# Nine attention steps of a fused attention and expert kernel: outputs placed one step later, between the next step's transposes and scores

## The chip, the cores and the metric

The kernel runs on one core of one Trainium2 chip. The metric is the device time in microseconds (us) of one execution, as the median of several runs. The engines are named as in the profile: PE is TensorE (its weight loads are PEld), DVE is VectorE, ACT is ScalarE, POOL is GpSimd, SP is SyncE, which issues most of the DMAs.

## The reference

Attention over 4 batches, 8 heads, 768 tokens and a head size of 64; each token sees the keys less than 16 places away and one summary key (a maximum) and one summary value (a mean) for each block of 32 tokens. Behind it stands a network on the 3072 tokens with 512 features each.

```python
k_sum = k.reshape(B, H, nb, block, D).max(axis=3)
v_sum = v.reshape(B, H, nb, block, D).mean(axis=3)
scores_all = np.concatenate([scores_l_m, scores_s], axis=-1)   # local with a mask, summaries + log(32)
a = np.exp(scores_all - max); a = a / (sum(a) + 1e-9)
attn = np.matmul(a, np.concatenate([v, v_sum], axis=2))
x = attn as (3072, 512)
h = (x @ w1) * (x @ w2) @ w3
out = h @ w_out
```

## The kernel before

**Two kinds of work share the core.** The attention is cut into 24 *steps*: 6 units of 512 tokens times 4 pairs of heads, step s being unit s // 4 and pair s % 4. The network is a long *stream* of matmuls of 128x512 (the *big* matmuls), which a generator hands out in order; `run(columns)` issues them until a given count of columns is reached. In the profile they are `mm` (L167) until about 245 us and `ln` (L731) from then on. The weights of the `ln` part are loaded into tiles `ws` (L776, L861, L867), some of them sums of weights that the kernel itself works out (`wr`, `sp`, cast by ACT at L682) and writes to DRAM (`wS`, `pS`, L688).

**A step of attention.** PE multiplies queries and keys into two PSUM banks, one for each head: `sc`, 32 small matmuls (L408). DVE adds the mask and takes the maxima (`reduce`, L422). ACT takes the exponential with the sums (`expose`, L436), then the inverse and `normalize` (L446). PE transposes the result `sm` into two banks `tp`, 16 small matmuls (L466). `evacuate` copies them into SBUF as `pt`: the first by ACT (L471), the second by ACT (L473), in two lumps by DVE (L475). PE multiplies `pt` by the values `v` into one bank `po`, 32 small matmuls (L486), and ACT copies that out as `xraw` (L507), or as `x` for the first 8 steps.

**PSUM.** Banks are handed out by tags, in turns. The tag `sc` has four: the scores take two, `po` takes one (`SPARE`, L457), and from lump 16 on `tp` takes two as well (L1176), since the two `tp` banks then belong to the stream. A new tile in a bank waits until the tile before it there has been read.

**A lump.** The first 8 steps are started by a plan written by hand (`PLAN`). The others go by `lump(p)`, p from 8 to 25 (L1168), which mixes three steps into a share of the stream. For p at its middle values a lump holds, in the order of PE: the transposes of step p−2; the scores of step p; 18 big matmuls; the outputs of step p−2; the rest of its big matmuls, up to `UP_TO[p]`. The order of PE and POOL is the written one; for ACT and DVE the written order holds among the attention instructions (the `manual_schedule` of L1177 and L1188), and a scheduler places those of the stream between them; SP is placed by the scheduler.

**Loads of a step.** `fetch(p + 1)` loads queries and keys (L373, L375). `fetch_values(p)` (L1199), behind the outputs of step p−2, loads the values of step p (`v`, L358), and the next lump's `fetch_means` (L1174) adds the means of the blocks (`v<-vS`, L391).

Of the kernel before, what the change touches and what calls it, by code (L numbers as in the profile page):

```python
# [91 lines left out]

HOMES = "TSTSTTTT"
BANKS = "STTTSTST"
SOONER = 400
RING = 5

# [18 lines left out]
def attention_moe(ctx, tc, qG, kW, kT, vP, vW, vB, mask, w1, w2, w3T, wo, out, outT):  # L116
# [52 lines left out]
    def aligned(shape, **more):  # L169


        n = math.prod(shape[1:])
        step = 32 if more["bufs"] % 4 == 0 else 64
        t = sb.tile([shape[0], -(-n // step) * step], F32, **more)[:, :n]
        return t.rearrange("p (a b) -> p a b", b=shape[2]) if len(shape) == 3 else t
# [85 lines left out]
    def fold_weights(order):  # L261
        acc = {}
        for i, j in order:
# [15 lines left out]
            def store(i=i):  # L279
                done = acc.pop(i)[:, :DO]  # L280
                with tc.high_priority(offset=SOONER):
                    nc.scalar.copy(wp[i][:, 0], done)
# [64 lines left out]
    def batches(u):  # L347

        for b in range(B):
            at, to = max(0, b * BLOCKS - u * NBLK), min(NBLK, (b + 1) * BLOCKS - u * NBLK)  # L350
            if at < to:
                yield b, slice(at, to), to - at

    def load_values(u, p):


        v = sb.tile([P, 2, NBLK, P], F32, name="v", bufs=2)
        nc.sync.dma_start(v, vW[u, p])  # L358
        return v
# [27 lines left out]
    def fetch_means(u, p, v):  # L387
        for b, blocks, n in batches(u):
            for g, at in enumerate((CUT, CUT - 64)):
                src = vS[b][32 * p : 32 * p + NB]  # L390
                nc.sync.dma_start(v[at : at + NB, g, blocks], src.unsqueeze(1).broadcast_to([NB, n, P]))  # L391
# [7 lines left out]
    def scores(q, k):  # L399

        sc = [ps.tile([P, 512], F32, name="sc", bufs=4) for _ in range(2)]
        for i in range(NBLK):
            for g in range(2):
                for h in range(2):
                    rows = slice(h * D, (h + 1) * D)
                    nc.tensor.matmul(  # L408
                        sc[h][64 * g : 64 * g + 64, i * KR : (i + 1) * KR],
                        lhsT=q[rows, i * P + 64 * g : i * P + 64 * g + 64],  # L410
                        rhs=k[rows, i, 64 * g : 64 * g + KR],
                        start=True,
                        stop=True,
                    )
        return sc
# [41 lines left out]
    SPARE = {"tag": "sc", "bufs": 4}  # L457

    def transposes(sm, **more):

        tp = [ps.tile([P, 512], F32, name="tp", **more or {"bufs": 2}) for _ in range(2)]
        for j in range(NI):
            for g in range(2):
                rows = slice(64 * g, 64 * g + 64)
                to, p = tp[g][:KR, j * 64 : j * 64 + 64], sm[rows, j]
                nc.tensor.transpose(to, p, ident[rows, rows])  # L466
        return tp

    def evacuate(tp, second="V"):
        pt = [sb.tile([KR, U], F32, name="pt", bufs=6) for _ in range(2)]  # L470
        nc.scalar.copy(pt[0], tp[0][:KR, :U])  # L471
        if second == "A":
            nc.scalar.copy(pt[1], tp[1][:KR, :U])  # L473
        else:
            nc.vector.tensor_copy(pt[1], tp[1][:KR, :U])  # L475
        return pt

    def outputs(pt, v, **more):

        po = ps.tile([P, 512], F32, name="po", **more or {"tag": "tp", "bufs": 2})  # L480
        for i in range(NBLK):
            for g in range(2):
                at = (2 * i + g) * 64
                for h in range(2):
                    cols = slice(h * D, (h + 1) * D)
                    nc.tensor.matmul(  # L486
                        po[cols, at : at + 64],
                        lhsT=v[:KR, g, i, cols],
                        rhs=pt[g][:, (h * NBLK + i) * 64 : (h * NBLK + i + 1) * 64],
                        start=True,  # L490
                        stop=True,
                    )
        return po
# [34 lines left out]
    def gate(fs, x, hs, wide=False):  # L528
# [5 lines left out]
        for c0, c1 in parts:  # L534
            for f in fs:
                k, cols = f * P // FQ, slice(f * P % FQ, f * P % FQ + P)
                for w in range(2):
# [14 lines left out]
                    if w == 0 and c1 == NC:  # L552
                        g = sb.tile([P, U], F32, name="g", tag="pt", bufs=6)
                        with tc.high_priority(offset=SOONER):
                            nc.scalar.copy(g, a)  # L555
                if c1 == NC:
                    if f % 2 == 0:
                        pair_of_h[0] = sb.tile([P, 2, 2, U], F32R, name="h", tag="ring", bufs=RING)
                    h = pair_of_h[0][:, f % 2]
                    with tc.high_priority(offset=SOONER):  # L560
                        nc.vector.tensor_tensor(g, acc[f, 1][:, :U], g, ALU.mult)
# [5 lines left out]
    def project(u, ts, hs, parts):  # L567
        acc = {t: ps.tile([P, 512], F32, name="mm", **bank(u == 1)) for t in ts}
        for fs in parts:
            for t in ts:  # L570
# [10 lines left out]
                if f == NF - 1:  # L581
                    o = sb.tile([P, DO], F32, name="o", tag="pt", bufs=6)
                    with tc.high_priority(offset=SOONER):
                        nc.scalar.copy(o, acc[t][:, :DO])
# [5 lines left out]
    NS = NU * NPAIR  # L590
# [125 lines left out]
    def lanes(n, o, weights_of, moving_of, steps, evacuated, tags, between=None, last=None):  # L716

        banks = [ps.tile([P, 512], F32, name="ln", tag=tag, bufs=bufs) for tag, bufs in tags]
        for at, k in enumerate(o.ids):
            stationary_of = yield from weights_of(at, k)  # L720
            for i in range(n):
# [3 lines left out]
                for c in range(steps):  # L725
# [13 lines left out]
                    if c < steps - 1:  # L739
                        yield 3 * U  # L740
                with tc.high_priority(offset=SOONER):
                    evacuated(at, k, i, banks[i][:, :U])
# [128 lines left out]
    def project_fast(n, whole):  # L871
        parts = []

        def between(at, j):
            with tc.high_priority(offset=SOONER // 2):
                if j < 3 and at + 2 < NK:
                    for work in whole.moving(at + 2):
                        next(work, 0)
            if n + 1 < NSU and j == 3 and at in (4, 5):
                moving_x(n + 1, at - 4)  # L880
# [99 lines left out]
    def tend():  # L980


        some = False
        for works in (tasks, background):
            while works:
                n = next(works[0], 0)
                if n > 0:
                    return True
                if n < 0:
                    break  # L990
                works.pop(0)
                some = True
        return some

    def run(columns):

        while given[0] < columns:
            n = next(stream, 0)
            if n <= 0:
                if n == 0 or not tend():  # L1000
                    return
                continue
            given[0] += n
            if given[0] >= tended[0]:
                tended[0] = given[0] + 4 * U
                tend()

    def place(s):
        return divmod(s, NPAIR)

    inputs, values, sms = {}, {}, {}
# [5 lines left out]
    def fetch_values(s):  # L1017
        if s < NS:
            values[s] = load_values(*place(s))
# [9 lines left out]
    def begin(s):  # L1029
        u, p = place(s)  # L1030
        sm = sb.tile([P, NI, KR], F32, name="sm", tag="wf", bufs=5)
        mx = aligned([P, 3, NI], name="mx", bufs=4)
        sms[s] = sm, mx
        return u, sm, mx, scores(*inputs.pop(s))
# [47 lines left out]
    def step(s):  # L1082
# [11 lines left out]
        yield  # L1094
        pt = evacuate(transposes(sms.pop(s)[0], **(SPARE if BANKS[s] == "S" else {})), SECOND[s])
        yield
# [40 lines left out]
    def finish_step(p, pt, **more):  # L1137
        u, c = place(p)
        po = outputs(pt, values.pop(p), **more)
        if u < 2:  # L1140
            keep_x(po, xs[u])
        else:
            keep_raw(po, u, c)
# [14 lines left out]
    for p in range(2 * NFIRST + 2, NS + 2):  # L1158
# [6 lines left out]
        15: [lambda: flow_in(4), lambda: moving_x(1, 2)],  # L1165
        17: [lambda k=k: moving_x(1, k) for k in range(3, NK)],
    }
    def lump(p):  # L1168

        if p == NFIRST:  # L1170
            load_batch()
            fill(p)
        elif p <= NS:
            fetch_means(*place(p - 1), values[p - 1])  # L1174
            fetch(p + 1)
        more = SPARE if p >= 2 * NFIRST else {}  # L1176
        with tc.manual_schedule(engines={engines.Activation, engines.DVE}):  # L1177
            tp = transposes(sms.pop(p - 2)[0], **more)
            pt = evacuate(tp, 'V' if p in (12,13,) else 'A')
            b = begin(p) if p < NS else None  # L1180
            if b:
                u, sm, mx, sc = b
                reduce(u, 0, sc, sm, mx)
                if p > NFIRST + 1:
                    expose(0, sm, mx)
                    reduce(u, 1, sc, sm, mx)
        run(given[0] + (24 if p == NFIRST + 1 else 18) * U)
        with tc.manual_schedule(engines={engines.Activation, engines.DVE}):  # L1188
            finish_step(p - 2, pt, **SPARE)
            if b:  # L1190
                if p <= NFIRST + 1:
                    expose(0, sm, mx)
                    reduce(u, 1, sc, sm, mx)
                expose(1, sm, mx)
                invert(mx)
                normalize(sm, mx)
            fill(p + 1)
            reduce_batch()
        fetch_values(p)  # L1199
        for work in EXTRA.get(p, ()):  # L1200
            work()
        run((given[0] + UP_TO[p]) / 2)
        load_batch()
        run(UP_TO[p])

    with tc.manual_schedule(engines=MANUAL):
        for p in range(NFIRST, NS + 2):
# [70 lines left out]
```

## Time and profile before

| | us |
|---|---|
| median of 3 runs | 505.18 |
| lowest and highest of them | 504.29, 505.75 |
| profiled execution, its own time | 507.58 |
| span of the profiled execution | 505.8 |

The mean granted clock of TensorE was 0.993 of full speed. The page gives the busy time of each engine over the span and the share of each in the chain that ended last. The chain is a list of pieces (start, duration, engine, tile and line); where PE is never idle, it is PE's own row of work. Lump 8 and the following ones begin where `tp` stands in it: lump 12 at 197.88 us, 16 at 243.93, 17 at 253.83, 20 at 300.12, 21 at 314.85, 22 at 330.32, 25 at 374.87; behind them comes only the stream.

### The profile page before, as it was taken

What the parts mean: (1) busy time and instruction counts of PE and PEld (TensorE: products, weight loads), DVE (VectorE), ACT (ScalarE), POOL (GpSimd) and SP (SyncE); (2) the same over time, 40 slices, a digit from 0 to 9 for tenths busy, and PEclk for the clock granted to TensorE, in tenths of its full rate; (3) what the DMA queues carried; (4) which work ended last, traced back from release to release, by engine and by line L of the source; (5) the groups of instructions that cost most, each with busy time, mean ns of one, the idle gap of its engine ahead of it and who ended that gap; (6) DMA issues with size and microseconds to landing.
All of it is one profiled execution on the core that took longest, in us unless ns stands there. A gap on an engine that the chain in (4) does not pass through costs nothing.

```text
span 505.8 us, 10295 instructions
## 1 busy us (share of the span) xinstructions
PE 487.9 (96%) x3756; PEld 391.7 (77%) x3756; DVE 366.3 (72%) x885; ACT 325.2 (64%) x890; POOL 43.8 (9%) x78
## 2 busy tenths in 40 slices
PE   1989999999999999999999999999999999999997
PEld 1658777888877777778777788777887888888886
DVE  5888987896845698994689865589977029129972
ACT  4977888893726788887897478547865421422710
POOL 2014301511320001000000000000000000000000
PEclk9979999999999999999999999999999999999999
DMA  8999769994975788899789877796858765656752
GB/s 319 407 398 358 279 230 404 409 399 191 319 279 173 266 278 278 270 327 364 262 287 328 294 288 224 289 329 182 250 192 243 225 192 190 202 180 200 212 186 101
DMA packets 52146, 136.65 MB, mean 270 GB/s; under 512 B 5120, under 2 KB 16128, under 8 KB 51072
## 3 DMA queue, kind: packets, MB, share of 16 engines
q1 hardware_dynamic: 50944, 133.90, 76.1%
q10 hardware_dynamic: 1152, 2.10, 1.1%
q8 instruction: 30, 0.49, 0.4%
q14 instruction: 20, 0.16, 0.1%
HBM read 107.47 MB, written 28.51 MB: 269 GB/s over the span
## 4 chain that ended last, share of the span: by engine, by line
PE 89%; ACT 4%; DMA 4%; DVE 1%; issue 0%; SPq 0%; DVEq 0%; ACTq 0%
PE ln L731 46%; PE mm L167 31%; PE po L486 5%; PE sc L408 4%; PE tp L466 3%; DMA wraw<-in_wo_dram 2%; DMA wS<-sp 2%; ACT wf L216 1%; DMA v<-in_vW_dram 1%; ACT wraw L224 1%; ACT w L246 1%; PE ln L167 1%; PE means L335 1%; ACT sm L446 0%; ACT sm L452 0%
## 5 line engine op out<-in xcount | busy, mean ns | idle before, releaser
L731 PE MATMUL ln<-xT,ws 128*128 128x512 f32 x672 | 157.1, 392 | 0.0
L731 PEld LDWEIGHTS ln<-xT,ws 128*128 128x128 f32 x672 | 124.9, 188 | 27.7 <-issue 1.1
L167 PE MATMUL mm<-x,w 128*128 128x512 f32 x384 | 91.9, 395 | 0.8 <-ACT g L555 0.8
L167 PEld LDWEIGHTS mm<-x,w 128*128 128x128 f32 x384 | 70.8, 188 | 17.8 <-ACT g L555 1.2
L436 ACT ACTIVATE sm<-sm,mx 128x120 f32<-128x120 f32 x192 | 73.9, 390 | 9.1 <-DVE mx L422 8.9
L731 PE MATMUL ln<-hT,ws 128*128 128x512 f32 x324 | 75.6, 392 | 0.0
L751 DVE TENSOR_TENSOR tmp<-ln,tmp 128x512 f32<-128x512 f32 x51 | 35.1, 688 | 52.0 <-PE ln L731 37.7
L731 PEld LDWEIGHTS ln<-hT,ws 128*128 128x128 f32 x324 | 60.3, 188 | 12.9 <-DVE hT L163 0.2
L167 PE MATMUL mm<-w,w 128*128 128x512 f32 x192 | 51.5, 422 | 13.5 <-ACT w L246 9.0
L650 ACT CAST hT<-hr 128x512 fp32r<-128x512 f32 x56 | 32.1, 621 | 42.7 <-DVE hr L808 35.1
L167 PEld LDWEIGHTS mm<-w,w 128*128 128x128 f32 x192 | 37.8, 202 | 24.4 <-ACT w L246 9.8
L422 DVE CUSTOM_DVE_ANT_0 sm<-sc,mask_sb 128x120 f32<-128x120 f32 x192 | 42.3, 277 | 7.4 <-PE sc L408 7.3
L167 PE MATMUL mm<-wp,h 128*128 128x512 f32 x192 | 46.0, 394 | 0.0
L446 ACT ACTIVATE sm<-sm,mx 128x120 f32<-128x120 f32 x128 | 39.0, 389 | 6.1 <-DVE mx L442 6.1
L167 PEld LDWEIGHTS mm<-wp,h 128*128 128x128 f32 x192 | 35.5, 188 | 8.0 <-issue 0.5
L163 DVE TENSOR_TENSOR hT<-hr,hT 128x512 fp32r<-128x512 f32 x56 | 35.5, 685 | 7.1 <-ACT hT L650 6.8
L436 ACT ACTIVATION_READ_ACCUMULATOR sm<-sm,mx 128x1 f32 x192 | 37.0, 192 | 0.0
L395 POOL COPY k<-ks 128x96 f32<-128x96 f32 (+1 forms) x32 | 13.5, 435 | 226.7 <-DMA k<-in_kW_dram 189.8
L486 PEld LDWEIGHTS po<-pt,v 120*64 120x64 f32 x768 | 24.5, 138 | 8.0 <-issue 4.5
L163 DVE TENSOR_TENSOR sp<-wr,sp 128x512 fp32r<-128x512 f32 x24 | 16.5, 696 | 16.7 <-ACT sp L682 16.6
L216 ACT ACTIVATE wf<-wraw 128x1024 f32<-128x1024 f32 (+1 forms) x24 | 23.4, 984 | 7.2 <-DMA wraw<-in_wo_dram 5.1
L486 PE MATMUL po<-pt,v 120*64 120x64 f32 x768 | 27.7, 225 | 0.2 <-ACT pt L473 0.2
(67 smaller groups left out, 570.5 us busy)
## 6 DMA issues: line engine op xcount, KB each, us to landing
ws<-wS SPq DMA_DIRECT2D x56, 512.0 KB
v<-in_vW_dram SPq DMA_DIRECT2D x24, 512.0 KB
wraw<-in_w_dram SPq DMA_DIRECT2D x8, 1024.0 KB
wS<-sp SPq DMA_DIRECT2D x16, 512.0 KB
ws<-pS SPq DMA_DIRECT2D x16, 512.0 KB
k<-in_kW_dram SPq DMA_DIRECT2D x20, 368.0 KB
wraw<-in_w3T_dram SPq DMA_DIRECT2D x7, 1024.0 KB
raw<-in_kT_dram SPq DMA_DIRECT2D x16, 392.0 KB
```

Of the source, the lines that this page charges most:

```text
L163: eng.tensor_tensor(dst, src, hi.bitcast(F32), ALU.subtract)
L167: nc.tensor.matmul(acc, lhsT=a, rhs=b, start=first and i == 0, stop=last and i == len(terms) - 1)
L216: nc.scalar.activation(f[:, some], words[:, some, 1].bitcast(F32), AF.Prelu, scale=2.0**-112, alpha=-(2.0**32),)
L408: nc.tensor.matmul(sc[h][64 * g : 64 * g + 64, i * KR : (i + 1) * KR], lhsT=q[rows, i * P + 64 * g : i * P + 64 * g + 64], rhs=k[rows, i, ...
L422: nc.vector.tensor_tensor_reduce(out=sm[:, j], in0=sc[h][:, i * KR : (i + 1) * KR], in1=mask_sb[:, 0 if blk == 0 else 2 if blk == BLOCKS - ...
L436: nc.scalar.activation(sm[:, j], sm[:, j], AF.Exp, bias=mx[:, 0, j : j + 1], scale=-1.0, accum_out=mx[:, 1, j : j + 1])
L446: nc.scalar.activation(sm[:, j], sm[:, j], AF.Copy, scale=mx[:, 2, j : j + 1])
L466: nc.tensor.transpose(to, p, ident[rows, rows])
L486: nc.tensor.matmul(po[cols, at : at + 64], lhsT=v[:KR, g, i, cols], rhs=pt[g][:, (h * NBLK + i) * 64 : (h * NBLK + i + 1) * 64], start=Tru ...
L650: nc.scalar.copy(dst[0], src)
L731: nc.tensor.matmul(banks[i][:, :U], lhsT=x, rhs=y, start=c + j == 0 and k in o.first, stop=c == steps - 1 and j == 2 and k in o.last, skip ...
L751: nc.vector.tensor_tensor(parts[to], got, parts[more], ALU.add)
```

## The change

`MERGED` names nine steps: 9 to 13 and 16 to 19. For these `lump(s + 2)` makes the transposes and `pt` as before, but keeps `pt`; the outputs are made in `lump(s + 3)`, behind that lump's transposes and copies and ahead of its scores. The other steps from 8 on (8, 14, 15, 20 to 23) and the last two of the first eight, 6 and 7, keep their place in the middle of the lump. So lump 11 and lump 18 have no outputs; lump 16 has those of step 13 at its start and of step 14 in its middle; lump 22 those of step 19 and of step 20. `fetch_values(s + 2)` follows the lump part in which step s was finished, so the values of steps 11 to 15 and 18 to 21 are loaded a lump later; the list `fresh` has the means follow at the start of the next lump.

```diff
+MERGED = (9, 10, 11, 12, 13, 16, 17, 18, 19)
...
+    fresh, kept_for_later = [], {}
+
     def lump(p):
...
-            fetch_means(*place(p - 1), values[p - 1])
+            while fresh:
+                s = fresh.pop(0)
+                fetch_means(*place(s), values[s])
             fetch(p + 1)
         more = SPARE if p >= 2 * NFIRST else {}
+        finished = []
         with tc.manual_schedule(engines={engines.Activation, engines.DVE}):
             tp = transposes(sms.pop(p - 2)[0], **more)
             pt = evacuate(tp, 'V' if p in (12,13,) else 'A')
+            if p - 3 in kept_for_later:
+                finish_step(p - 3, kept_for_later.pop(p - 3), **SPARE)
+                finished.append(p - 3)
             b = begin(p) if p < NS else None
...
         run(given[0] + (24 if p == NFIRST + 1 else 18) * U)
         with tc.manual_schedule(engines={engines.Activation, engines.DVE}):
-            finish_step(p - 2, pt, **SPARE)
+            if p - 2 in MERGED:
+                kept_for_later[p - 2] = pt
+            else:
+                finish_step(p - 2, pt, **SPARE)
+                finished.append(p - 2)
...
-        fetch_values(p)
+        for s in finished:
+            fetch_values(s + 2)
+            if s + 2 < NS:
+                fresh.append(s + 2)
```

On PE the two lumps 19 and 20 stood like this before (each row is a run of like matmuls: line, output and inputs, shape, count):

```order
L466 MATMUL tp<-ident,sm 120x64 x16
L408 MATMUL sc<-k,q 64x120 x16
L731 MATMUL ln<-xT,ws 128x512 x18
L486 MATMUL po<-pt,v 64x64 x16
L731 MATMUL ln<-xT,ws 128x512 x36
L466 MATMUL tp<-ident,sm 120x64 x16
L408 MATMUL sc<-k,q 64x120 x16
L731 MATMUL ln<-xT,ws 128x512 x18
L486 MATMUL po<-pt,v 64x64 x16
L731 MATMUL ln<-xT,ws 128x512 x33
```

and stand like this now, all lines being one higher up to the lump:

```order
L467 MATMUL tp<-ident,sm 120x64 x16
L487 MATMUL po<-pt,v 64x64 x16
L409 MATMUL sc<-k,q 64x120 x16
L732 MATMUL ln<-xT,ws 128x512 x54
L467 MATMUL tp<-ident,sm 120x64 x16
L487 MATMUL po<-pt,v 64x64 x16
L409 MATMUL sc<-k,q 64x120 x16
L732 MATMUL ln<-xT,ws 128x512 x51
```

The outputs have moved ahead of the scores, and the two runs of big matmuls have become one; the big matmuls are the same, in the same order. (These lists show 16 for the 32 matmuls that the profile counts in sc and po.)

In lump 16 PE has these waits now, at the end of tp and at the start of po and of sc (numbers tell tiles apart; the square brackets name what the instruction waits for):

```order
L467 MATMUL tp_3046<-ident_64,sm_2758 120x64
L487 MATMUL po_3067<-pt_2896,v_2836 64x64 [waits DMAHW2_49,DMAHW5_49,DVE_49,PE_49]
...
L409 MATMUL sc_3087<-k_2873,q_2872 64x120 [waits DMAHW4_49,DMAHW7_49,Activation_49,Pool_49]
L409 MATMUL sc_3088<-k_2873,q_2872 64x120 [waits Activation_49]
L409 MATMUL sc_3087<-k_2873,q_2872 64x120
L409 MATMUL sc_3088<-k_2873,q_2872 64x120
```

The second scores matmul waits for ACT's copy of the first tp tile of the same lump, whose bank it takes; it has the same wait in lumps 19 to 22. On ACT, from the end of lump 20 to the middle of lump 21, this was the order before:

```order
L441 ACTIVATE mx<-mx 128x8
L446 ACTIVATE sm<-sm,mx 128x120 x8
L682 CAST sp<-wr 128x512
L471 COPY pt<-tp 120x512
L473 COPY pt<-tp 120x512
L682 CAST sp<-wr 128x512
L436 ACTIVATE sm,mx<-sm,mx 128x120 x4
L507 COPY xraw<-po 128x512
L436 ACTIVATE sm,mx<-sm,mx 128x120 x4
```

and this is it now:

```order
L442 ACTIVATE mx<-mx 128x8
L447 ACTIVATE sm<-sm,mx 128x120 x8
L683 CAST sp<-wr 128x512 x2
L472 COPY pt<-tp 120x512
L474 COPY pt<-tp 120x512
L508 COPY xraw<-po 128x512
L437 ACTIVATE sm,mx<-sm,mx 128x120 x8
```

Both casts of `sp` now stand ahead of the two copies, and the copy of po stands ahead of the exponentials instead of between them. The first of the two casts overwrites a tile whose DMA to `pS` must have landed.

## The prediction

> **What bounds the kernel now.** I read the page first: how busy each engine is, the granted clock, and by what the chain that ended last is made up.
>
> ```profile
> PE 487.9 (96%) x3756; PEld 391.7 (77%) x3756; DVE 366.3 (72%) x885; ACT 325.2 (64%) x890; POOL 43.8 (9%) x78
> ...
> PEclk9979999999999999999999999999999999999999
> ...
> PE 89%; ACT 4%; DMA 4%; DVE 1%; issue 0%; SPq 0%; DVEq 0%; ACTq 0%
> ```
>
> TensorE (PE) is busy 96% of the span at full clock and makes 89% of the chain. The next question is whether it waits anywhere near the changed steps. The view of PE's waits from 120 to 400 us has one row:
>
> ```profile
> PE mm L167 <- ACT g L555: 0.8, 1, 0.8
> ```
>
> One wait of 0.8 us; from there to the last matmul PE runs on. So in the changed stretch time can only be won by making PE's own row of work shorter, and each wait that the change gives PE lengthens the kernel one for one. What PE does in a lump is in the chain (start, duration, what); here are lump 16 (its tp at 243.93), the po of lump 17, the second half of lump 19, lump 20 and the end:
>
> ```profile
> 243.93 0.61 PE tp L466 x16
> ...
> 249.87 1.08 PE po L486 x32
> 250.95 2.94 PE ln L731 x12
> ...
> 259.84 1.08 PE po L486 x32
> ...
> 291.73 8.38 PE ln L731 x36
> 300.12 0.61 PE tp L466 x16
> 300.73 0.98 PE sc L408 x32
> 301.71 4.34 PE ln L731 x18
> 306.06 1.08 PE po L486 x32
> 307.14 7.70 PE ln L731 x33
> 314.85 0.61 PE tp L466 x16
> ...
> 380.89 118.69 PE ln L731 x522
> ```
>
> A lump is transposes (tp), scores (sc), 18 big matmuls, outputs (po), and the rest of the big matmuls, each starting where the last ended. Two runs behind po differ only in length: 36 take 8.38 us, 12 take 2.94 us, so one big matmul costs (8.38 − 2.94) / 24 = 0.2267 us, and a run behind po has 8.38 − 36 × 0.2267 = 0.22 us more than its matmuls. The run behind sc has 4.34 − 18 × 0.2267 = 0.26 us more. I call this the edge: what it costs PE to go between small and big matmuls.
>
> **The change part by part.** *The merged run.* In nine lumps po leaves the middle of the big matmuls and goes between tp and sc. No matmul is removed. Two runs (4.34 + 8.38 = 12.72 us) become one of 54: 54 × 0.2267 + 0.26 = 12.50 us. That saves 0.22 us a step and 9 × 0.22 = 1.98 us in all.
>
> *What po costs in its new place.* It has tp ahead of it and sc behind it. The early part of the program has one of these two edges:
>
> ```profile
> 51.63 1.08 PE po L486 x32
> 52.71 0.98 PE sc L408 x32
> 53.70 2.27 PE mm L167 x9
> ```
>
> Here po with sc behind it takes 1.08 us and sc 0.98 us, as elsewhere, so that edge adds nothing. tp with po behind it is not in this trace. Its bounds: nothing, or the idle time that the weight loads show where PE goes from sc to big matmuls, 0.16 us:
>
> ```profile
> 301.64 3.99 PEld L731 LDWEIGHTS ln<-xT,ws 128*128 128x128 f32 x18 [0.16 <-issue]
> ```
>
> So the saving of a step lies between 0.22 − 0.16 = 0.06 and 0.22 us, or 0.5 to 2.0 us for nine. I take 0.22, since small matmuls follow one another in the nearest row (po to sc) without a price.
>
> *A new wait for PSUM banks.* The tag "sc" has four banks. From lump 16 on tp takes two of them, sc two and po one, five in a lump. Before, the order tp, tp, sc, sc, po let po come round to the first bank of tp, long after its copy. With tp, tp, po, sc, sc it is the second scores bank that comes round to the first bank of tp of the same lump, and its first matmul, the second of the scores, waits until ScalarE (ACT) has copied it out (L471). What covers this is po itself, 1.08 us: the copy must have ended 0.61 + 1.08 = 1.69 us after tp starts. It concerns lumps 16, 19, 20, 21 and 22. Where ACT is free, the copy starts right behind tp, as in lump 21 (the last row here); in lumps 16 and 20 (the rows before) ACT came to it late:
>
> ```profile
> 244.03 0.56 ACT L584 COPY o<-mm 128x512 f32<-128x512 f32 x1
> ...
> 246.23 0.34 ACTq L585 DMA_DIRECT2D out_dram<-o  x1
> 246.61 0.59 ACT L471 COPY pt<-tp 120x512 f32<-120x512 f32 x1 [0.57 <-DMA out_dram<-o]
> ...
> 300.15 0.59 ACT L749 COPY tmp<-ln 128x512 f32<-128x512 f32 x1 [0.48 <-PE ln L731]
> 300.64 0.62 ACT L650 CAST hT<-hr 128x512 fp32r<-128x512 f32 x1
> 301.16 0.59 ACT L471 COPY pt<-tp 120x512 f32<-120x512 f32 x1
> ...
> 315.49 0.58 ACT L471 COPY pt<-tp 120x512 f32<-120x512 f32 x1 [0.67 <-PE tp L466]
> ```
>
> Lump 21's copy starts 0.64 us after tp (315.49 against 314.85) and would end 0.47 us in time; lumps 19 and 22 look the same in ACT's order. Lump 20's ends at 301.75, 1.63 us after tp's start: in time by 0.06 us, so I put 0 to 0.1 there and take 0.05. In lump 16 the copy ended 3.3 us after tp's start at 243.93. In the new order the normalisations stand ahead of the output copy o (L584), so after tp's start there are the last o (begins 0.10 us after it, lasts 0.56), the issue of its DMA (0.57 of idle time) and the copy (0.59): 0.10 + 0.56 + 0.57 + 0.59 = 1.82 us against 1.69. That is 0.13 us late if the normalisations are done by then, and up to 1.6 us (3.3 − 1.69) if they are as late as before. I take 0.4 us, nearer to the low end, because ACT no longer waits for po in the middle of a lump, as it did here:
>
> ```profile
> 337.39 0.59 ACT L507 COPY xraw<-po 128x512 f32<-128x512 f32 x1 [3.12 <-PE po L486]
> ```
>
> *The Trainium skill, page "TensorEngine Tiling (Array Packing)", section "PSUM Bottleneck", says that packing small matmuls speeds TensorE but not the emptying of PSUM, so that the copy out of PSUM may become the bottleneck.* By it every one of the five bank waits would decide; by the rows only those decide where ACT comes late, since a copy of 0.58 us is shorter than the 1.08 us that cover it.
>
> *ACT behind a DMA in lump 21.* Before, ACT copied both pt and then stood before a cast for the network's weights; in the new order two such casts stand ahead of the copies. The first overwrites a buffer whose write to DRAM must have landed. Before, that was this wait, and this was the DMA's issue:
>
> ```profile
> 314.20 0.62 ACT L682 CAST sp<-wr 128x512 fp32r<-128x512 f32 x1 [0.84 <-PE ln L731]
> ...
> 320.14 0.62 ACT L682 CAST sp<-wr 128x512 fp32r<-128x512 f32 x1 [3.57 <-DMA pS<-sp]
> ```
>
> ```profile
> 311.46 0.80 SPq L776 DMA_DIRECT2D ws<-wS  x2
> 312.37 0.37 SPq L688 DMA_DIRECT2D pS<-sp  x1
> ```
>
> It landed 320.14 − 312.37 = 7.8 us after its issue, behind a load of v and two of weights. In the new order the same cast and DMA come earlier, and only the one write of the same kind stands directly ahead of it, not the weights. I estimate its issue about 1.8 us earlier, 310.6 on the clock of before, when the DMA engines have room:
>
> ```profile
> 308.00:310.00 2.00, 2.00 (x11) 1.64 (x10) 0.00 (x0) 2.00 (x9) 0.00 (x0) 1.00 0.66 258
> ...
> 314.00:320.00 6.00, 6.00 (x68) 4.72 (x67) 1.35 (x2) 1.69 (x3) 0.00 (x0) 1.00 0.95 327
> ```
>
> (The last two columns are the DMA engines' share and GB/s: 0.66 there, 0.95 in the 6 us behind.) Behind the wait on ACT's queue stand two casts (0.51 us from start to start: 300.64 to 301.16) and the copy, and PE's scores wait for the copy. So the landing must come by 314.85 + 1.69 − 0.59 − 2 × 0.51 = 314.93, which is 4.3 us after the issue. The fastest landing of this kind that ended a wait of ACT is here, 210.96 − 207.43 = 3.5 us:
>
> ```profile
> 207.43 0.33 SPq L688 DMA_DIRECT2D wS<-sp  x1
> ```
>
> ```profile
> 210.96 0.62 ACT L682 CAST sp<-wr 128x512 fp32r<-128x512 f32 x1 [0.42 <-DMA wS<-sp]
> ```
>
> With 3.5 us nothing is lost, with 7.8 us 3.5 us are. I take 0.4 us, a landing of 4.7 us, since fewer bytes stand ahead than in the case of 7.8 us.
>
> *The rest, at nothing.* A v load still stands two lumps ahead of its use, but for step 15: loaded when lump 16 has begun and used in the middle of lump 17, some 16 us (243.93 to 259.84). The slowest landing above is 7.8 us, so 8 us of cover stay; if they were gone, po would wait for v and PE with it. SP's copies v<-vS move a lump later with the loads, and stand behind a load that is then a lump old. The scores' reductions on VectorE (DVE) start 1.08 us later; they are needed by tp two lumps on, some 22 us at the least (two lumps of 11 us, the first row below). DVE is busiest in lumps 12 and 13:
>
> ```profile
> 198.00:209.20 11.20, 11.20 (x116) 8.86 (x116) 11.12 (x34) 9.61 (x33) 2.00 (x2) 1.00 0.78 256
> 209.20:221.20 12.00, 12.00 (x120) 9.55 (x119) 11.65 (x33) 9.97 (x36) 0.08 (x1) 1.00 0.86 272
> ```
>
> (The third figure behind the stretch is DVE's busy time, 11.12 of 11.20 us.) Its other work slips by the same 1.08 us at most, and one wait of that kind cost 0.8 us in the first view. Outputs left in PSUM until the next lump need no bank: the copied pt is what is kept, in six buffers.
>
> *The sum.* −1.98 + 0.4 (lump 16) + 0.4 (lump 21) + 0.05 (lump 20) = −1.13 us. The profiled execution took 507.58 us, span 505.8, and would take 506.45; the median of the runs is 505.18, 2.40 us below it, and gives 505.18 − 1.13 = 504.05, said as 504.1 us. About 0.3%, or 1.5 us, is what a measurement of this kernel can tell from no change; the forecast lies within it.
>
> **The rivals.** *A, the forecast:* small bank waits in lumps 16 and 21 take 0.5 to 1.3 us of the 1.98: 503.7 to 504.5 us.
>
> *B, all copies come in time:* lump 16's by the earlier normalisations, lump 21's by a landing under 4.3 us. The gain is 1.5 to 2.0 us: 503.2 to 503.7 us. For it: ACT is only 64% busy and two of three terms are just at their point. Against it: in lump 16 the sum of rows is over the point by 0.13 us even so.
>
> *C, slower, by ACT's queue in lump 21:* the write lands after 7.8 us as before, because SP issues it no earlier; it decides from 4.3 us on. It costs 3.5 us; with lump 16's 0.4 us and the gain of 1.98 this is 505.18 + 1.9 = 507.1 us, 506.8 to 508.3 us with lump 16's whole range. For it speaks that the same wait was 3.57 us before; against it, the room in the DMA view.
>
> *D, it does not do what it says:* the new edge of tp and po takes 0.16 us, the saving is 0.5 us in all, or each of the five bank waits costs 0.4 us and takes 2.0 us back. 504.7 to 505.5 us. The Trainium skill's rule above on the emptying of PSUM is this case's second half. For it: no row of before shows tp and po together; against it, the two lumps where ACT stands idle before the copy.
>
> **How the numbers follow.** A 0.38, B 0.38, C 0.14, D 0.10. A and D lie within 0.3% (0.48); B, with 1.5 us or more, is faster (0.38); C is slower (0.14). A and B are as likely as each other, and the sum stands in A, hence 504.1 us. The range reaches over B, A and D, with the scatter of the runs on the low side, 503.0, and into the beginning of C, with landings of up to 6 us (505.18 − 1.98 + 0.4 + 1.7 = 505.3 and the scatter), 506.0. It leaves out most of C.
>
> **What would show it right or wrong.** In the chain of the changed kernel one run of 54 big matmuls of about 12.50 us should stand where 4.34 and 8.38 us stood; if it is 12.7, the edge was misread. tp should take 0.61 us with po behind it; 0.77 is D. The view of PE's waits should show sc waiting for pt (L472) in lump 16, some tenths, and perhaps in lump 21; in lumps 19 and 22 nothing. A wait of more than 2 us there, with ACT's cast waiting for the write of sp, is C. A wait of po for v, or of a big matmul for DVE, would make the steps costed at nothing wrong.

## The result, and the profile after

The changed kernel takes 508.17 us (median of 6 runs, 506.96 to 508.5); the kernel before, run beside it, 504.74 us (6 runs). The ratio is 1.0064 with a 95% interval of 1.0047 to 1.0082: 3.4 us slower, where 1.1 us faster was forecast. A second set of 12 runs, told below, gives 506.77 us and 1.0039 [1.0021, 1.0056].

The two profiled executions don't show this in their totals. The one of before took 507.58 us, far above its median, the one of after 506.96, the fastest of its six. They differ ahead of any change: the transposes of lump 10 start at 174.56 us in the one, at 172.24 in the other, though up to 190 us every engine has the same instructions in the same order in both. So I compare lumps, each from the start of its transposes to the start of the next one's (us, worked out from PE's timeline):

| lump | before | after | after, second trace | a copy on DVE (below) |
|---|---|---|---|---|
| 11 | 12.01 | 10.70 | 10.70 | 10.70 |
| 12 | 11.32 | 11.07 | 11.06 | 11.07 |
| 13 | 12.01 | 11.74 | 11.75 | 11.74 |
| 14 | 11.33 | 11.07 | 11.07 | 11.07 |
| 15 | 11.32 | 11.07 | 11.06 | 11.07 |
| **16** | **9.97** | **14.77** | **15.49** | **11.12** |
| 17 | 15.41 | 15.41 | 15.41 | 15.40 |
| 18 | 15.40 | 14.10 | 14.10 | 14.10 |
| 19 | 15.41 | 15.14 | 15.14 | 15.15 |
| 20 | 14.73 | 14.52 | 14.52 | 14.51 |
| 21 | 15.48 | 15.39 | 15.14 | 15.20 |
| 22 | 14.72 | 15.77 | 15.78 | 15.77 |
| lumps 10 to 24 | 200.24 | 201.89 | 202.36 | 198.04 |

Lumps 11 and 18 have lost their outputs, lumps 16 and 22 have two; the others that changed are 0.2 to 0.3 us shorter. One row is out of order: lump 16 should have grown by one po and its edges, to about 11 us, and is at 14.77. From lump 10 to 24 the two traces of after are 1.65 and 2.12 us longer than before. That is the loss of the second set of runs (0.39%, 2.0 us); the 3.4 us of the first set are some 1.5 us more. The intervals of the two sets overlap; what the executions without a trace lost beside lump 16 is not known.

First the merged runs, in the chain of waits of after (start, duration, what):

```profile
271.05 12.51 PE ln L732 x54
283.56 0.61 PE tp L467 x16
284.17 1.08 PE po L487 x32
285.25 0.98 PE sc L409 x32
286.23 12.47 PE ln L732 x54
...
300.40 1.03 PE sc L409 x32
...
314.91 1.23 PE sc L409 x32
```

The run of 54 takes 12.47 to 12.51 us, tp with po behind it 0.61, po 1.08: the new edges cost nothing. The scores of lump 20 lose 0.05 us, those of lump 21 0.25.

Now lump 16. The view of PE's waits from 120 us on has one row in after (us in total, times, longest), and one of 2.4 us in the second trace:

```profile
PE sc L409 <- ACT pt L472: 1.7, 1, 1.7
```

```profile
PE sc L409 <- ACT pt L472: 2.4, 1, 2.4
```

The chain of the first leaves PE there and goes back through ACT to a load:

```profile
233.70 8.23 DMA q<-in_qG_dram
...
242.01 0.35 ACTq L586
242.37 0.04 issue
242.41 0.59 ACT pt L472
243.00 0.04 issue
243.05 1.04 PE sc L409 x30
244.09 5.93 PE ln L732 x18
```

ACT's own timeline says why:

```profile
239.88 0.56 ACT L585 COPY o<-mm 128x512 f32<-128x512 f32 x1
242.01 0.35 ACTq L586 DMA_DIRECT2D out_dram<-o  x1
242.41 0.59 ACT L472 COPY pt<-tp 120x512 f32<-120x512 f32 x1 [1.97 <-DMA q<-in_qG_dram]
```

The output tile o was copied by 240.44. Its DMA, issued by ACT, went out only at 242.01, when a load of q had landed that SP had issued at 233.70, 8.2 us earlier. That load has nothing to do with o: in the program the output's DMA waits for the semaphore that counts the landing of this load,

```order
L586 DMA out_0_dram<-o_3034 128x512 [waits DMAHW7_49,Activation_49]
```

and the program's DMAs share the names DMAHW0 to DMAHW7 in turns. Behind the issue stands the copy of tp, and behind the copy PE's scores. The loss has a second half: the 18 big matmuls behind the wait take 5.93 us instead of 4.34. The windows (length, PE's busy time and matmuls, then the granted clock, the DMA engines' share, GB/s) say what that is:

```profile
240.00:242.00 2.00, 1.32 (x34) 1.00 1.03 404
242.00:244.00 2.00, 0.95 (x30) 1.00 0.92 203
244.00:245.00 1.00, 1.00 (x7) 0.84 0.84 299
245.00:246.00 1.00, 1.00 (x4) 0.50 1.05 418
246.00:247.00 1.00, 1.00 (x4) 0.50 1.00 394
247.00:248.00 1.00, 1.00 (x4) 0.50 1.07 421
248.00:250.00 2.00, 2.00 (x11) 0.98 0.94 368
```

From about 244.7 us on, 1.6 us after the wait has ended, PE is granted half its clock for 3.4 us (the windows together have lost 1.7 us of full clock). Of the 3.8 us that lump 16 is too long (14.77 against the 11.01 that it takes in two kernels below without a wait), 1.6 us (5.93 − 4.34) are the clock and 2.2 us the gap; the row of waits says 1.73, and the first two scores matmuls ahead of it are drawn with another 0.4 us.

### The profile page after: what moved, and what is told of

Same layout as the page of the kernel before. It is cut to its first block, busy times and chain, and to the rows that moved or that the text cites. A ratio compares the mean times of both kernels' runs of the same rounds, so it can differ in the third digit from the quotient of the medians.

```text
span 505.1 us, 10288 instructions
## 1 busy us (share of the span) xinstructions
PE 486.4 (96%) x3756; PEld 393.3 (78%) x3756; DVE 367.0 (73%) x885; ACT 326.1 (65%) x890; POOL 43.0 (9%) x78
## 4 chain that ended last, share of the span: by engine, by line
PE 91%; ACT 3%; DMA 3%; DVE 1%; issue 0%; SPq 0%; ACTq 0%; DVEq 0%
PE ln L732 46%; PE mm L168 32%; PE po L487 5%; PE sc L409 4%; PE tp L467 3%; DMA wraw<-in_wo_dram 2%; DMA q<-in_qG_dram 2%; ACT wf L217 1%; ACT wraw L225 1%; ACT w L247 1%; PE ln L168 1%; PE means L336 0%; ACT sm L453 0%; DVE wf L242 0%; DVE w L164 0%
## 5 line engine op out<-in xcount | busy, mean ns | idle before, releaser
L732 PEld LDWEIGHTS ln<-xT,ws 128*128 128x128 f32 x672 | 126.4, 189 | 27.8 <-issue 1.1
L750 ACT COPY tmp<-ln 128x512 f32<-128x512 f32 x32 | 18.8, 587 | 17.1 <-PE ln L732 17.0
```

The costliest lines, as they stand in the source:

```text
L732: nc.tensor.matmul(banks[i][:, :U], lhsT=x, rhs=y, start=c + j == 0 and k in o.first, stop=c == steps - 1 and j == 2 and k in o.last, skip ...
L750: nc.scalar.copy(parts[to], got)
```

## The experiments

**Theory 1:** lump 16 holds the whole loss: the bank wait, behind ACT's wait to issue a DMA, and the half clock behind it. **Theory 2:** the loss is spread over the changed stretch, by later value loads and later reductions. **Theory 3**, formed later: ACT would be late in lump 16 by its own work, whatever its DMA waits for. Each kernel was run beside the kernel before; the ratio is to its runs.

**Step 13 left out** (lump 16 keeps the old order):

```diff
-MERGED = (9, 10, 11, 12, 13, 16, 17, 18, 19)
+MERGED = (9, 10, 11, 12, 16, 17, 18, 19)
```

> The change with step 13 taken out of the nine, so that lump 16 keeps the old order (transposes, scores, 18 big matmuls, outputs). Theory 1 (the loss is one place: in lump 16 the second scores bank waits for ACT's copy of tp, which stands behind ACT's wait to issue an output DMA, 1.7 us, and the clock granted behind that idle time is 0.5 for 3 us, another 1.6 us): no wait of PE for pt in lump 16, clock 1.00 there, and eight steps at about 0.24 us less 0.3 us of waits in lumps 20 and 21, so 1.6 us faster than before, about 503.1. Theory 2 (the loss is spread over the changed stretch: later value loads and later reductions cost DMA or DVE time in many lumps): still slower than before, 507 or more.

503.79 us against 504.74, ratio 0.9985 [0.9970, 0.9999]; lump 16 took 9.96 us. Theory 2 falls: with eight of the nine steps still moved the loss is gone. The gain is short of the 1.6 us. In this trace lump 21 took 16.29 us, by the wait that the prediction had put there:

```profile
311.27 1.14 ACT L683 CAST sp<-wr 128x512 fp32r<-128x512 f32 x2 [1.31 <-DMA pS<-sp]
312.31 0.58 ACT L472 COPY pt<-tp 120x512 f32<-120x512 f32 x1
```

The casts of sp waited for their tile's write to land; the copy and PE (0.73 us) waited behind them.

**Step 13 alone:**

```diff
-MERGED = (9, 10, 11, 12, 13, 16, 17, 18, 19)
+MERGED = (13,)
```

> Only step 13 is moved. Theory 1: one merged run won (0.24 us), and the wait in lump 16 with the low clock behind it in full if ACT is held as long by the load that its output DMA has to wait for (another load than in the changed kernel): 1 to 3.3 us slower than before, 506 to 508. Theory 2: one ninth of the loss, within 0.4 us of before.

505.72 us against 504.74, ratio 1.0004 [0.9984, 1.0025]: the loss that theory 1 expected is not in the runs; the interval reaches from 0.8 us faster to 1.3 us slower. So either ACT is not held as long in most executions, which was theory 1's condition, or theory 2 is right; this comparison alone doesn't tell which. The other eleven runs lie wide apart, 502.8 to 507.7 us, and four of them have a mean granted clock of 1.00, so in these it hardly fell anywhere. The traced execution is longer than any of them, 511.58 us, and stands for itself alone:

```profile
244.89 0.34 ACTq L586 DMA_DIRECT2D out_dram<-o  x1
245.27 0.59 ACT L472 COPY pt<-tp 120x512 f32<-120x512 f32 x1 [3.07 <-DMA raw<-in_vB_dram]
```

Here the output's DMA waits for another load, PE waits 3.15 us, and lump 16 takes 17.17 us.

**Steps 9 to 12 alone**, twice:

```diff
-MERGED = (9, 10, 11, 12, 13, 16, 17, 18, 19)
+MERGED = (9, 10, 11, 12)
```

> Only steps 9 to 12 are moved, all finished before lump 16, where tp has banks of its own tag. Theory 1: no bank wait of consequence, four merged steps at 0.24 us, 1.0 us faster, about 503.8. Theory 2: slower than before by about four ninths of the loss, 1.5 us, 506.3.

> Steps 9 to 12 alone once more, because the trace of the first look was 1.2 us shorter than before between lump 10 and the last run of big matmuls while the runs' median was 0.5 us longer. Theory 1: the trace holds, the median comes out 0.5 to 1.2 us below before, 503.6 to 504.3. Theory 2 (moves in the classic lumps cost something in most executions): above before again, and the trace shows a wait of PE between 180 and 240 us or in the part ahead of it.

First 505.28 against 504.74, 1.0007 [0.9990, 1.0024]; then 505.25 against 505.19, 1.0008 [0.9983, 1.0033]. The gain of 1.0 us is not in the times. In the first trace it is: lumps 12, 13 and 14 as in after, lumps 10 to 24 in 199.14 us against 200.24, and no wait of PE. In the second they take 202.33 us, with these waits of PE:

```profile
PE ln L732 <- DVE hr L752: 1.7, 1, 1.7
PE ln L732 <- DVE mx L423: 0.9, 1, 0.9
```

They stand in lumps 18 and 21 (16.63 and 17.38 us), not between 180 and 240 us as theory 2 would have it. The one in lump 21 goes back to a write of sp, in the chain:

```profile
311.59 6.35 DMA pS<-sp
318.02 0.63 ACT sp L683
...
320.42 7.78 PE ln L732 x33
```

So in both traces the gain was made, and in the second it was lost again in lumps that this kernel doesn't change (from 250 us on its engines have the same order of instructions as before). That before loses as much there in some of its executions is likely, but it has one trace alone. Why the runs' medians show no gain stays open.

**The output DMAs issued by SP:**

```diff
-nc.scalar.dma_start(out[u * U + t * P : u * U + (t + 1) * P], o)
+nc.sync.dma_start(out[u * U + t * P : u * U + (t + 1) * P], o)
```

> All nine steps moved as in the change, but the DMAs of the output tiles o are issued by SP instead of ACT, so ACT no longer waits for another DMA ahead of the copies of tp. Theory 1: in lump 16 the copy follows the output copy at once, PE waits there for 0 to 0.3 us, the clock stays at 1.00, 1.5 to 2 us faster than before, about 503.2. Theory 2: as slow as the change, 508.

509.19 against 504.74, 1.0083 [1.0063, 1.0103], a miss by the time. By place it is not: lump 16 took 11.01 us, without a wait. The loss has moved to 149 us, where the first unit's outputs are written (the chain, and PE's longest wait):

```profile
145.78 0.34 SPq L586
...
146.70 4.14 DMA v<-in_vW_dram
...
153.10 1.88 PE sc L409 x32
```

```profile
PE sc L409 <- POOL k L396: 4.0, 1, 4.0
```

SP now waits for the copy of o, and a load of v stands behind that: it goes out at 146.70, in after at 137.42. POOL waits for its landing with copies into v, its gather of k stands behind these, and PE's scores wait 4.0 us for the gather; the clock was 0.50 from 151.0 to 157.8 us. So the next run moves only the second unit's outputs:

```diff
-nc.scalar.dma_start(out[u * U + t * P : u * U + (t + 1) * P], o)
+(nc.sync if u else nc.scalar).dma_start(out[u * U + t * P : u * U + (t + 1) * P], o)
```

> All nine steps moved and every copy of tp on ACT as in the change; only the four output DMAs of the second unit, of which the last stands ahead of lump 16's copies on ACT, are issued by SP. Theory 1 (ACT stands there because the output DMA may not be issued before a load of q has landed): lump 16 about 11.0 us with no wait of PE, 1.5 to 2 us faster than before, as with the copy on DVE. Theory 3 (ACT would be late in lump 16 anyhow, by its own work): a wait of 0.3 us or more stays there.

504.0 against 505.22, 0.9975 [0.9953, 0.9998]. With all copies of tp on ACT as in the change, lump 16 falls from 14.77 to 11.44 us, and ACT copies tp right behind o:

```profile
241.25 0.56 ACT L585 COPY o<-mm 128x512 f32<-128x512 f32 x1
241.72 0.57 ACT L472 COPY pt<-tp 120x512 f32<-120x512 f32 x1
```

The copy ends at 242.29, 2.08 us after tp's start at 240.21, so 0.4 us late, and 0.43 us is what the lump is above 11.01. That much is theory 3: here o begins 1.04 us after tp's start, behind ACT's normalisations. The rest is ACT's wait for the DMA. Lump 21 took 17.03 us in this trace, again behind the landing of sp's write.

**Only the copy moved:** in lump 16 the first copy of tp goes to DVE.

```diff
-nc.scalar.copy(pt[0], tp[0][:KR, :U])
+if first == "A":
+    nc.scalar.copy(pt[0], tp[0][:KR, :U])
+else:
+    nc.vector.tensor_copy(pt[0], tp[0][:KR, :U])
...
-pt = evacuate(tp, 'V' if p in (12,13,) else 'A')
+pt = evacuate(tp, 'V' if p in (12,13,) else 'A', 'V' if p == 16 else 'A')
```

> All nine steps moved as in the change; only in lump 16 the first copy of tp goes to DVE, which is idle there, so that the second scores bank no longer waits for ACT and its output DMA. Theory 1 (lump 16 holds the loss): lump 16 falls from 14.77 to about 11.0 us in the trace, clock 1.00 there; 508.2 less 3.7 us, about 504.4, or 503.2 if the nine merged runs give their 2.0 us in full. Theory 2 (the loss is spread, and lump 16 is only where it shows in one execution): 507 or more.

503.44 against 505.19, ratio 0.9964 [0.9945, 0.9983]: 1.8 us faster than before, the lowest ratio of all kernels here. Lump 16 takes 11.12 us, 0.11 above 11.01: DVE is not idle there, as the expectation had it, but sums values until 240.0 us, 1.1 us after tp began. ACT still stands before its output DMA, and PE doesn't wait for it:

```profile
239.77 0.56 ACT L590 COPY o<-mm 128x512 f32<-128x512 f32 x1
241.54 0.35 ACTq L591 DMA_DIRECT2D out_dram<-o  x1
241.93 0.59 ACT L479 COPY pt<-tp 120x512 f32<-120x512 f32 x1 [1.59 <-PE sc L409]
```

(The added code moves the lines, L479 here is L474 in after. The releaser in the brackets is inferred; the issue at 241.54 is the one before it.) This confirms theory 1 from the other side: not ACT's wait is dear, but that the scores' bank hangs on it.

**Steps 16 to 19 alone:**

```diff
-MERGED = (9, 10, 11, 12, 13, 16, 17, 18, 19)
+MERGED = (16, 17, 18, 19)
```

> Only steps 16 to 19 are moved. Theory 1: lumps 18 to 22 as in the changed kernel, 4 times 0.25 us won and 0 to 0.9 us lost in lump 21 behind the DMA of sp: 0.1 to 1.0 us faster, 503.7 to 504.6. Theory 2: slower than before by four ninths of the loss, 506.2.

504.46 against 505.19, 0.9987 [0.9969, 1.0004], by the middle 0.7 us faster, as theory 1 had it, though the interval reaches no change. Lumps 18 to 22 are as in the last column of the table.

**What a wait costs.** On the kernel with DVE's copy, the first copy of tp is made five times in lump 19 and seven times in lump 22:

```diff
+for _ in range(again):
+    nc.scalar.copy(pt[0], tp[0][:KR, :U])
...
-'V' if p == 16 else 'A')
+'V' if p == 16 else 'A', {19: 4, 22: 6}.get(p, 0))
```

> The kernel with lump 16's copy on DVE, and the first copy of tp made five times over in lump 19 and seven times over in lump 22, each time the same data; the scores wait for the last of them. With 0.48 us a copy and 0.46 us of slack PE should wait 1.5 us in lump 19 and 2.4 us in lump 22. If the clock is lowered by idle time of PE alone: 2.4 us is followed by 3 us or more at 0.50 and costs lump 22 another 1.7 us; the 1.5 us lies between the 0.99 us that did not lower it and the 1.73 us that did, and tells where the point lies. If the low clock of lump 16 had another cause there (DMA at its limit): clock 1.00 in both, and each wait costs its own length.

509.69 against 505.19, 1.0107 [1.0066, 1.0148]. PE waited 1.72 and 2.95 us, somewhat longer than expected. Lump 19 grew by 2.16 us (17.31 against 15.15), its gap alone; lump 22 by 4.96 us (20.73 against 15.77), the gap of 3.4 us (2.95 and the 0.41 of the first two matmuls) and 1.6 us of half clock. Windows behind the longer and the shorter wait:

```profile
331.90:333.30 1.40, 1.40 (x32) 0.94 0.17 67
333.30:336.50 3.20, 3.20 (x9) 0.50 0.35 109
336.50:338.00 1.50, 1.50 (x8) 0.98 0.54 182
283.40:287.00 3.60, 3.60 (x41) 1.00 0.57 206
```

The clock fell with the DMA engines at 0.17 to 0.35, so the DMA load of lump 16 is not needed for it; idle time of PE was enough in this execution. Not in every one: another of the six runs (507.83 us) has a mean granted clock of 1.00, so there neither wait lowered it (of that run there is no trace).

**More steps moved.** Twelve steps, and then all from 8 to 21, on the kernel with DVE's copy. Both leave out the loads of the means for step 23, whose values come a lump too late for the list; that is two small DMAs, 38 of this kind in their traces against 40.

```diff
-MERGED = (9, 10, 11, 12, 13, 16, 17, 18, 19)
+MERGED = (8, 9, 10, 11, 12, 13, 16, 17, 18, 19, 20, 21)
```

> Lump 16's copy on DVE, and steps 8, 20 and 21 moved as well, twelve in all. If a merged run is worth 0.24 us wherever no copy is late: another 0.7 us, 502.6 to 502.9 if the kernel with nine gives 503.4. If the later lumps have a late copy, a wait of PE in lump 23, 24 or 25 eats it: 503.4 or more.

```diff
-MERGED = (9, 10, 11, 12, 13, 16, 17, 18, 19)
+MERGED = tuple(range(8, 22))
...
-'V' if p == 16 else 'A'
+'V' if p in (16, 17, 18, 21) else 'A'
```

> All steps from 8 to 21 moved, with the first copy of tp on DVE in lumps 16, 17, 18 and 21. If every copy is in time: 14 times 0.24 us, 3.4 us faster than before, 501.8. In lump 17 ACT is 3 us late and DVE has a product and a cast's remainder ahead of the copy; if it comes late too, PE waits there for DVE, and over 1.7 us the clock may fall: 504 or more.

515.82 and 524.29 us against 505.22, 1.0195 [1.0164, 1.0226] and 1.0378 [1.0350, 1.0406]. By both times a late copy ate the gain. PE's waits of the first and, in the second fence, the two longest of the other:

```profile
PE sc L409 <- ACT pt L473: 6.1, 1, 6.1
PE sc L409 <- DVE pt L475: 2.6, 1, 2.6
```

```profile
PE sc L409 <- DVE pt L475: 9.3, 2, 6.9
PE sc L409 <- ACT pt L473: 6.1, 1, 6.1
```

Every new place with a late copy is such a wait: ACT in lump 23 behind nine casts of hT and eight normalisations (343.57 to 350.54 us in the first), DVE in lump 16 behind the sums of the values, and in lump 18 of the second behind sums of weights. One of them did not lower the clock, the 2.44 us in lump 16 of the second:

```profile
241.10 1.04 PE L409 MATMUL sc<-k,q 64*64 64x120 f32 x30 [2.44 <-DVE pt L475]
```

```profile
242.00:246.00 4.00, 4.00 (x23) 1.00 0.97 327
```

**The change once more:**

> The change once more, since its first trace was one of its fastest executions. Theory 1: lump 16 again 14 to 16 us, with a gap of 2 us or more ahead of the scores and a clock of 0.50 behind it, 3 us slower than before. Theory 2: lump 16 near 11 us while the time is still 3 us longer.

506.77 against 505.22, 1.0039 [1.0021, 1.0056]; in the trace a wait of 2.42 us and lump 16 at 15.49 us. The loss of 2.0 us is smaller than the 3 us expected.

How often the clock falls in lump 16, the runs' mean clocks can't tell. A stretch of 3.4 us at half clock takes 0.0034 off the mean, and the trace of after has one near 30 us too (its mean clock from 29 to 34 us is 0.66). Of these 12 runs seven have 0.992 or 0.993 (506.7 to 509.1 us) and five 0.997 (506.3 to 506.8); of the first six, five have 0.992 or 0.993. None of the 18 has 1.00, which 8 of the 23 runs of before beside them have. That fits a half clock in lump 16 in each of the 18, but only two traces show it.

## Why the prediction was wrong, by its own steps

*What bounds the kernel:* right. The waits of PE compared here were paid in full, and some more than once.

*The merged run, 0.22 us a step:* right, slightly small. Lumps 12 to 15 and 19 show 0.25 to 0.27, lump 20 0.21; all nine in the kernel with DVE's copy 200.24 − 198.04 = 2.20 us, against 1.98. (Of these some 0.07 us are a wait that lump 21 had before, 15.48 us against 15.41 for its like, and no longer has.) Its runs, 1.8 us faster, lie where case B put them, 1.5 to 2.0.

*The new edge of tp and po:* nothing, as taken.

*The bank wait:* the mechanism and its five lumps were right, with nothing in 19 and 22 and 0.05 us in lump 20, as said. **The step that failed is the sum for lump 16**, "0.10 + 0.56 + 0.57 + 0.59 = 1.82 us against 1.69", and the 0.4 us, at most 1.6, made of it. Two of its terms were mis-sized. The 0.57 us was taken as the price of issuing the output DMA, but the row that it was read from names a landing as its end, [0.57 <-DMA out_dram<-o]; there the landing came just after ACT had finished its other work (idle from 246.04 us on, the issue at 246.23). In the new order of the DMAs ACT is held until a load of q lands: from the end of o's copy to the copy of tp it took 1.97 us, and 2.56 in the second trace (issues at 242.01 and 242.62, both against 240.44). And o begins 0.67 us after tp's start (239.88 against 239.21), not 0.10, since the normalisations are not done by then. So the sum is 0.67 + 0.56 + 1.97 + 0.59 = 3.79 us, 2.1 us late. Without the hold (the second unit's outputs by SP) lump 16 loses 0.43 us; that this is the forecast's 0.4 is luck, since there o comes 1.04 us late and no issue stands on ACT. And a third term was missing: nothing stood for what follows a gap, 1.6 us of half clock. Together 3.8 to 4.5 us, more than the whole gain.

*ACT behind the write of sp in lump 21:* right as a range. 0.25 us in the first trace, none in the second, 1.1 us without step 13, 1.9 us with the second unit's outputs by SP; 0 to 3.5 was the bound, 0.4 the value. The sum of it was off in two ways that met halfway: the write goes out 3.28 us ahead of the lump's start (309.87 against 313.15), 0.9 us earlier than before and not the estimated 1.8, and it lands after 3.2 to 5.1 us in these four traces, 4.7 in the forecast.

*The rest at nothing:* no wait for v in the changed kernel, and none for DVE; the waits for DVE in the second trace with steps 9 to 12 show that this cover can be thin.

*The rivals:* the time came out where rival C put it, 506.8 to 508.3 us (the second set's 506.77 just below), by C's kind of mechanism, a DMA that holds ACT ahead of the copy. But C stood in lump 21 and priced a write of sp; in lump 16 ACT's DMA was counted as an issue, not as a wait. So that its number was met is luck. Of rival D neither half came: the edge cost nothing, and four of the five bank waits cost 0.3 us together. The Trainium skill, page "TensorEngine Tiling (Array Packing)", section "PSUM Bottleneck", says that, once TensorE is sped up, the copy out of PSUM may become the bottleneck; here it did in lump 16 alone.

## What to carry to other kernels

A DMA issue in an engine's queue can be a wait: before moving PE's consumer behind a copy, read what each DMA ahead of that copy waits for, its semaphore included, and not how long the issue took last time. Give a copy that PE will wait for to an engine with nothing ahead of it at that moment; which engine that is can change with the next step that is moved, as in lump 16 with twelve. And a gap in PE can cost more than its length: here one of 2.2 us cost 3.8, and another of the same length, in lump 19, only itself.

## What the runs showed of the hardware

The granted clock fell to 0.50 behind some gaps of PE and not behind others. As the profile lists them, waits of 0.73, 0.78, 0.99, 1.48, 1.69, 1.72 and 2.44 us left it at 1.00; waits of 1.73, 2.42, 2.58 and 2.95 us were followed by about 3.4 us at 0.50, and waits of 3.15 and 3.96 us by 6.8 us. (The 1.48 us stood in lump 21 with the second unit's outputs by SP, the 2.58 us in lump 16 with twelve steps.) It fell 1.9 to 4.3 us after the wait had begun, behind the first four when PE was at work again. The Trainium skill, page "TensorE: Matmul & The Clock Gate", section "HAM oscillation — how this bites in real kernels", gives the rule that PE should have no idle gaps over about 3.4 us. The runs here differ: a wait of 1.73 us was enough, and 1.72 and 2.44 us in other places were not. So between these it depends on more than the length; no run here shows on what.

A DMA of 256 KB, the load of q, took 8.2 us from issue to landing while the DMA engines were busy (1.03 in the first of the windows above), and through the shared semaphore this reached an engine that neither issued it nor used its data.
